# Gated linear attention and an MLP mixer on one core: another hand-over order for the same operations

## The chip, the cores and the metric

The kernel runs on one core of one Trainium2 chip. The metric is device microseconds (us) of one execution. A core has five engines that run side by side, each through its own list of instructions in order: TensorE (PE, matmuls; its weight loads are shown as PEld), ScalarE (ACT), VectorE (DVE), GpSimd (POOL) and SyncE (SP, which mostly issues DMAs). An engine whose next instruction waits for something stands still, and everything behind that instruction in its list stands still with it. Matmul results go to PSUM, which has eight banks; the other engines empty them into SBUF.

## The reference

Four sequences (batches) of 768 rows, 8 heads of width 48. First a gated linear attention, row by row, then an MLP mixer over its result (8 x 48 = 384 columns):

```python
f = 1.0 / (1.0 + np.exp(-f_logit))
for t in range(S):
    state = f[:, :, t, :, None] * state + np.einsum('bhd,bhe->bhde', k[:, :, t], v[:, :, t])
    y[:, :, t] = np.einsum('bhd,bhde->bhe', q[:, :, t], state)

x = y.transpose(0, 2, 1, 3).reshape(B, S, H * D)
h = np.maximum(x.transpose(0, 2, 1) @ w_tok1, 0.0) @ w_tok2       # 768 -> 256 -> 768, over rows
u = x + h.transpose(0, 2, 1)
h2 = np.maximum(u @ w_ch1, 0.0) @ w_ch2                            # 384 -> 1536 -> 384, over columns
out = u + h2
```

## The kernel before

**Tiling.** The 768 rows of a batch are cut into six chunks of 128. Two chunks are worked together (256 rows lie on 128 partitions, two neighbouring rows, j0 and j1, on each), so each batch has three *chunk pairs*, written b.P here: 1.2 is batch 1, chunk pair 2. For a pair the loop over rows becomes a few matmuls and elementwise steps:

1. gates: exp and ln of f on ACT (L449, L451), then `two` (and `two_lo` for b > 0) on DVE (L444)
2. running sums of ln f down a chunk on PE (L473 for b = 0, L475 and L476 after; called *sums*), chunk totals (L480, b = 0); `first` on DVE (L502); four exps of the sums into `GG` on ACT (L505 and L522); end-of-chunk decays (`glast`, L508; or `ends`, L512, and a small transfer on SP, L518)
3. *products*: q and k times `GG`, two per pair, j0 and j1 (L444, `qk<-qk_sb,GG`; DVE, for b = 0 also POOL)
4. *transposes* of the products: for b = 0 and 1 on PE (L550), then copied from PSUM to `qT` and `kT` by ACT or DVE (L430, L432); for b = 2 and 3 by DMA (L535), with a POOL copy (L434)
5. *scores* (L585), masked into `AmT` (DVE in one step, L628; for four tiles of batch 0 an ACT copy, L623, and a POOL multiply, L625)
6. *parts* k times v (L603), which carry the state from chunk to chunk on DVE (L637 to L645); the block-diagonal copy `state_bd` is cast by ACT, DVE or POOL
7. *outs*: state times q (L661) and `AmT` times v (L669) into PSUM, copied to `x_bf` (bf16) and `x_nat` (fp32). For batch 0 the three first `x_bf` tiles are cast late from `x_nat`, on POOL, ACT or DVE.

When a batch's rows are there, the mixer follows: L713 over rows into `h1T` (relu in two halves on ACT or DVE), L729 back, the residual u on DVE (L745), u's bf16 copy `u_bf`, its transposes (L770 on PE, L759 by DMA for b = 2 and 3), copied to `uT`; then the channel mix, L788 into `zT` (24 relus on ACT or DVE, L439 and L441) and L807, the sum (L813) and the store (L706). The mixer of one batch overlaps the attention of the next.

**What sets the order.** The kernel first records 1041 operations, each with the engines that may run it, its inputs and outputs and its PSUM bank. `Plan.best` then walks the table `ORDER` (L23 to L86): a code's quotient by 4 is the operation, its remainder says which of the allowed engines takes it. On the way it computes a planned start for each operation from costs, gives a PSUM bank to each group (the one that has been free longest), and, where PE would stand idle before 25.5 us, puts filler matmuls (L848, on `steady`) into its list. The operations are then emitted by planned start. So the table decides three things: the order in each engine's list, the engine of an operation that has a choice, and the banks. Waits follow from the data: an instruction waits for its inputs, for the readers of what it overwrites, and a group on a bank for those who empty it.

POOL issues the loads of q, k, v and f for the batches ahead (L358) and the weights (L365, L403) from the same list in which it casts and masks; a load that stands behind other work is issued late. At most two buffers hold f, three hold q, k and v.

Of the kernel before, what the change touches and what calls it, by code (L numbers as in the profile page):

```python
# [23 lines left out]
    8, 12, 0, 20, 24, 28, 4, 16, 244, 248, 252, 256, 140, 32, 44, 48, 36, 168, 120, 124, 132, 172, 40, 268, 128,  # L24
    56, 64, 272, 276, 416, 280, 148, 284, 288, 296, 300, 80, 84, 292, 420, 424, 432, 260, 164, 160, 72, 60, 68,
    304, 152, 308, 156, 76, 428, 88, 356, 360, 365, 369, 320, 312, 264, 325, 436, 372, 92, 96, 316, 564, 328,
    332, 376, 444, 448, 384, 380, 340, 568, 572, 580, 584, 588, 452, 348, 456, 336, 352, 100, 468, 473, 576,
    596, 592, 440, 104, 108, 460, 464, 600, 112, 116, 176, 180, 184, 188, 192, 344, 196, 388, 392, 508, 396,
    476, 480, 604, 512, 400, 408, 500, 488, 616, 621, 200, 404, 204, 492, 504, 413, 608, 521, 517, 484, 612,
    764, 524, 624, 628, 528, 532, 536, 496, 636, 632, 644, 648, 768, 736, 652, 740, 540, 544, 548, 656, 664,  # L30
    660, 640, 668, 672, 676, 553, 208, 557, 212, 684, 561, 681, 744, 772, 748, 752, 756, 776, 780, 784, 136,
    789, 760, 872, 856, 840, 844, 860, 876, 808, 812, 824, 828, 792, 796, 865, 848, 880, 920, 928, 816, 832,
    800, 884, 852, 912, 916, 925, 933, 888, 904, 896, 1248, 893, 1252, 836, 908, 820, 900, 1104, 1080, 1040,
    1032, 960, 1036, 1108, 1272, 952, 1044, 944, 1276, 869, 804, 144, 1280, 1284, 1120, 964, 1084, 948, 1125,
    1304, 1308, 1048, 1053, 1056, 1061, 957, 992, 936, 1024, 976, 1000, 1288, 1296, 1292, 1316, 940, 1028, 1312,
    981, 996, 1005, 984, 989, 1320, 1324, 1256, 1260, 1328, 1016, 968, 1096, 1088, 1332, 972, 1100, 1092, 1428,
    1432, 1021, 1436, 216, 1300, 220, 224, 228, 1440, 1460, 1464, 1448, 1444, 1336, 1340, 1344, 1348, 1352,
    1008, 1264, 1012, 1268, 1356, 1360, 1472, 1372, 1364, 1148, 1152, 1072, 1128, 1064, 1468, 1077, 1384, 1484,
    1476, 1112, 1380, 1452, 1068, 1376, 1488, 232, 236, 240, 688, 1588, 1592, 1596, 1604, 1608, 2264, 1368,
    1117, 1480, 1388, 1600, 1132, 1156, 1136, 1400, 1404, 1160, 1140, 1628, 692, 696, 700, 704, 1612, 2268,  # L40
    2288, 1408, 1420, 1424, 1624, 1620, 1412, 1396, 1392, 2272, 1416, 1492, 1496, 1500, 1504, 1508, 1456, 1616,
    1516, 2292, 1528, 1520, 1512, 1632, 1208, 1168, 1172, 1176, 1532, 2296, 1524, 1180, 2276, 2448, 1636, 1644,
    1536, 2304, 2308, 1640, 1544, 2312, 1648, 1540, 1560, 1564, 1212, 2300, 2452, 1548, 708, 712, 716, 720,
    1216, 1652, 1656, 1660, 1664, 1668, 1684, 1680, 1676, 1672, 1576, 1572, 1568, 1804, 1776, 1780, 2456, 1808,
    1784, 1812, 1188, 1552, 1580, 2324, 1556, 1816, 1788, 2320, 2472, 1700, 1704, 1688, 1692, 1696, 1584, 724,
# [836 lines left out]
```

## Time and profile before

| what | us |
|---|---|
| time, median of 3 runs | 168.66 (168.13 to 168.73) |
| the profiled execution, its own time | 168.51 |
| its span in the trace | 166.8 |
| busy: PE, DVE, ACT, POOL | 158.5, 129.3, 106.0, 63.5 |
| the two costliest lines: L807, L788 (both on PE) | 52.1, 50.3 |
| moved by DMA | 24.34 MB, mean 146 GB/s |

The trace names for each instruction its start, its duration, the engine and line, and how long its engine had been idle before it, with whoever ended that. Rows that follow each other without a gap on the same line are shown as one with their count. A row of the table by stretches gives for a stretch of the span the busy time of each engine and the number of its instructions. PE's rows may read as busy without a gap while it waits, because a matmul's end is modelled; the starts are recorded, so a wait shows as a start that comes later than the work before it needs.

The span has three stages: to about 32.8 us the attention of batch 0 and its row mix, with PE short of work; to about 72.2 the channel mix of batch 0 beside the attention of batch 1; then the channel mix of batches 1, 2 and 3 beside the attention of 2 and 3, which ends by about 130.

### The profile page before, as it was taken

What the parts mean: (1) busy time and instruction counts of PE and PEld (TensorE: products, weight loads), DVE (VectorE), ACT (ScalarE), POOL (GpSimd) and SP (SyncE); (2) the same over time, 40 slices, a digit from 0 to 9 for tenths busy, and PEclk for the clock granted to TensorE, in tenths of its full rate; (3) what the DMA queues carried; (4) which work ended last, traced back from release to release, by engine and by line L of the source; (5) the groups of instructions that cost most, each with busy time, mean ns of one, the idle gap of its engine ahead of it and who ended that gap; (6) DMA issues with size and microseconds to landing.
All of it is one profiled execution on the core that took longest, in us unless ns stands there. A gap on an engine that the chain in (4) does not pass through costs nothing.

```text
span 166.8 us, 5023 instructions
## 1 busy us (share of the span) xinstructions
PE 158.5 (95%) x2064; PEld 101.5 (61%) x2064; DVE 129.3 (78%) x287; ACT 106.0 (64%) x228; POOL 63.5 (38%) x87
## 2 busy tenths in 40 slices
PE   5899997899999999999999999999999999999991
PEld 2467865656666666566665766665667566566660
DVE  3499995889899998999999998996699446460331
ACT  3788975789899999976957939386531311725000
POOL 7975899705877200675517003024022022000000
PEclk9999999999999999999999999999999999999998
DMA  5999999999999991599999660985730043600253
GB/s 122 220 177 171 202 211 238 190 233 217 207 221 217 224 238 27 77 162 198 198 199 141 125 165 0 106 158 118 185 120 4 0 98 81 205 0 4 78 194 105
DMA packets 68183, 24.34 MB, mean 146 GB/s; under 512 B 60896, under 2 KB 67296, under 8 KB 68160
## 3 DMA queue, kind: packets, MB, share of 16 engines
q0 software_dynamic: 41856, 13.77, 67.6%
q1 hardware_dynamic: 25776, 10.06, 28.2%
q8 instruction: 16, 0.26, 0.6%
q10 hardware_dynamic: 528, 0.20, 0.4%
q14 instruction: 7, 0.06, 0.1%
HBM read 25.17 MB, written 4.72 MB: 179 GB/s over the span
## 4 chain that ended last, share of the span: by engine, by line
PE 75%; ACT 13%; DVE 5%; issue 2%; DMA 2%; DVEq 0%; ACTq 0%
PE ps L788 27%; PE ps L807 22%; PE ps L729 4%; PE ps L713 4%; PE ps L585 3%; PE ps L669 3%; ACT state_bd L430 2%; PE ps L661 2%; DMA f_sb<-in_f_logit_dram 2%; PE ps L603 2%; ACT f_sb L449 2%; ACT GG L522 2%; PE ps L550 2%; ACT f_sb L451 2%; ACT GG L505 1%
## 5 line engine op out<-in xcount | busy, mean ns | idle before, releaser
L807 PE MATMUL ps<-w_ch,zT 128*128 128x384 bf16 (+2 forms) x300 | 52.1, 320 | 0.4 <-ACT x_nat L430 0.4
L788 PE MATMUL ps<-uT,w_ch 128*128 128x384 bf16 x288 | 50.3, 326 | 0.1
L807 PEld LDWEIGHTS <-zT 128*128 128x128 bf16 x300 | 28.2, 98 | 17.7 <-issue 0.4
L788 PEld LDWEIGHTS <-w_ch 128*128 128x128 bf16 x288 | 27.7, 98 | 17.9 <-issue 0.3
L439 ACT ACTIVATE zT<-ps 128x384 bf16<-128x384 f32 x58 | 26.0, 495 | 16.9 <-PE ps L788 16.7
L628 DVE TENSOR_TENSOR AmT<-ps,mask 128x512 bf16<-128x512 f32 x44 | 28.3, 680 | 1.0 <-PE ps L585 0.8
L441 DVE TENSOR_SCALAR zT<-ps 128x384 bf16<-128x384 f32 x38 | 20.0, 552 | 6.1 <-PE ps L788 6.0
L813 DVE TENSOR_TENSOR x_nat<-x_nat,ps 128x384 f32<-128x384 f32 (+2 forms) x25 | 13.0, 532 | 10.3 <-PE ps L807 10.3
L434 POOL CAST state_bd<-state 48x192 bf16<-48x192 f32 x16 | 5.9, 369 | 33.0 <-DVE state L645 24.3
L444 DVE TENSOR_TENSOR qk<-qk_sb,GG 128x768 bf16<-128x768 bf16 x24 | 13.9, 585 | 1.2 <-ACT GG L522 1.1
L745 DVE TENSOR_TENSOR x_nat<-x_nat,ps 128x384 f32<-128x384 f32 x21 | 10.6, 548 | 3.9 <-PE ps L729 3.9
L358 POOL DMA_DIRECT2D v_sb<-in_v_dram x12 | 10.7, 888 | 5.7 <-DMA w_ch<-in_moe_w_ch_dram 4.9
L505 ACT ACTIVATE GG<-ps 128x384 bf16<-128x384 f32 x24 | 10.8, 488 | 3.1 <-DVE first L502 1.4
L522 ACT ACTIVATE GG<-first 128x384 bf16<-128x384 f32 x24 | 11.8, 520 | 0.6 <-DVE first L502 0.4
L449 ACT ACTIVATE f_sb<-f_sb 128x768 f32<-128x768 f32 x12 | 10.1, 845 | 2.9 <-DMA f_sb<-in_f_logit_dram 2.9
L848 PE MATMUL ps<-steady 128*128 128x512 bf16 x32 | 10.3, 444 | 1.7 <-DVE steady L373 1.7
L434 POOL COPY qT<-qJ 128x1024 bf16<-128x1024 bf16 x5 | 6.0, 1197 | 14.7 <-DMA qJ<-qk 14.6
L358 POOL DMA_DIRECT2D qk_sb<-in_k_dram x12 | 10.8, 900 | 2.0 <-POOLq L866 0.8
L430 ACT ACTIVATE u_bf<-x_nat 128x384 bf16<-128x384 f32 x13 | 6.0, 528 | 8.0 <-DVE x_nat L745 8.0
L358 POOL DMA_DIRECT2D qk_sb<-in_q_dram x12 | 10.6, 887 | 1.3 <-DMA qk_sb<-in_q_dram 0.7
L430 ACT ACTIVATE x_bf<-ps 128x384 bf16<-128x384 f32 x13 | 6.3, 490 | 6.2 <-PE ps L669 4.4
L713 PE MATMUL ps<-x_bf,w_tok 128*128 128x384 bf16 x48 | 10.1, 326 | 0.1
(84 smaller groups left out, 227.8 us busy)
## 6 DMA issues: line engine op xcount, KB each, us to landing
out_dram<-x_nat SPq DMA_DIRECT2D x23, 192.0 KB, 2.2
f_sb<-in_f_logit_dram POOLq DMA_DIRECT2D x9, 384.0 KB, 8.6
qk_sb<-in_k_dram POOLq DMA_DIRECT2D x12, 192.0 KB, 8.7
qk_sb<-in_q_dram POOLq DMA_DIRECT2D x12, 192.0 KB, 8.7
v_sb<-in_v_dram POOLq DMA_DIRECT2D x12, 192.0 KB, 8.8
w_ch<-in_moe_w_ch_dram POOLq DMA_DIRECT2D x2, 576.0 KB, 13.9
w_ch<-in_moe_w_ch_dram POOLq DMA_DIRECT2D x1, 1152.0 KB, 13.1
f_sb<-in_f_logit_dram SPq DMA_DIRECT2D x2, 384.0 KB, 5.6
```

Source lines behind the costliest of these rows:

```text
L358: lambda eng=eng, into=held(dst[i], P), of=runs(src, b, P): eng.dma_start(out=into, in_=of),
L430: nc.scalar.activation(out_, in_, AF.Copy, bias=0.0, scale=1.0)
L439: nc.scalar.activation(out_, in_, AF.Relu, bias=0.0, scale=1.0)
L441: nc.vector.tensor_scalar(out_, in_, 0.0, None, ALU.max)
L444: (nc.vector if op.engine == DVE else nc.gpsimd).tensor_tensor(out_, a, b_, what)
L449: add(ACT, r, lambda: nc.scalar.activation(fb, fb, AF.Exp, bias=0.0, scale=-1.0), make=[key], kind=el, need=([("fb", P)] if P < 1 else []) ...
L522: add(ACT, r, lambda n=n: nc.scalar.activation(GG[i][:, 0, n], banks[p_f.at][:, 0:DM].rearrange("t (h d) -> t h d", d=D) if split else fir ...
L628: add(DVE, r, lambda into=into, made=made, m4=m4: nc.vector.tensor_tensor(into, made(), m4, ALU.mult), need=masks, make=[("AmT", i, js, pa ...
L713: add(PE, rank("tok1", rt), lambda rt=rt, kt=kt, pm=pm: nc.tensor.matmul(banks[pm.at][:, 0:DM], lhsT=w_tok1[:, kt, rt * 128:(rt + 1) * 128 ...
L788: nc.tensor.matmul(banks[pm.at][:, 0:384], lhsT=w[:, kt, c0:c0 + 128], rhs=uT[:, th, :, kt, :], start=(kt == 0), stop=(kt == 2))
L807: nc.tensor.matmul(banks[pm.at][:, 0:n1 - n0], lhsT=zT[:, kt, tt * 128:(tt + 1) * 128], rhs=w_ch2[:, kt, n0:n1], start=(kt == 0), stop=(kt ...
L813: add(DVE, rank("ch2", tt), lambda un=un, pm=pm, n=n1 - n0: nc.vector.tensor_tensor(un, un, banks[pm.at][:, 0:n], ALU.add), make=[("x_nat" ...
```

## The change

Only the table `ORDER` differs, in all its 62 lines: it holds the same 1041 operations, in another order and in part with another choice of engine. A line of it says nothing to a reader:

```diff
 ORDER = (
-    8, 12, 0, 20, 24, 28, 4, 16, 244, 248, 252, 256, 140, 32, 44, 48, 36, 168, 120, 124, 132, 172, 40, 268, 128,
...
+    8, 12, 0, 20, 24, 28, 4, 16, 244, 248, 252, 256, 32, 160, 44, 48, 120, 140, 152, 156, 36, 40, 60, 132, 56,
...
 )
```

The planned starts move with it, and so the fillers: 32 before, 30 now. What each engine's list holds where the prediction speaks of it:

VectorE, the start of batch 0, before (`first_80` and `first_81` belong to chunk pairs 0.0 and 0.1, the two `qk_84` to 0.0's products):

```order
L502 TENSOR_TENSOR first_80<-ps_121,f_sb_74 128x384
L412 MEMSET state_bd_101 128x192
L415 MEMSET qk_84 128x2x8x8 x2
L394 TENSOR_TENSOR mask<-tri_114,ident 64x64 x2
L392 COPY mask<-tri_114 64x128
L444 TENSOR_TENSOR qk_84<-qk_sb_68,GG_82 128x2x8x48
L412 MEMSET state_bd_102 128x192
L444 TENSOR_TENSOR qk_84<-qk_sb_68,GG_82 128x2x8x48
L412 MEMSET state_bd_103 128x192
L396 COPY mask<-tri_114 64x64
L502 TENSOR_TENSOR first_81<-ps_122,f_sb_74 128x384
L637 TENSOR_TENSOR ps_123<-ps_123,glast_94 128x192
```

and now:

```order
L502 TENSOR_TENSOR first_80<-ps_121,f_sb_74 128x384
L415 MEMSET qk_85 128x2x8x8
L396 COPY mask<-tri_114 64x64
L502 TENSOR_TENSOR first_81<-ps_122,f_sb_74 128x384
L444 TENSOR_TENSOR qk_84<-qk_sb_68,GG_82 128x2x8x48 x2
L412 MEMSET state_bd_101 128x192
L637 TENSOR_TENSOR ps_123<-ps_123,glast_94 128x192
```

`first` of 0.1 has moved ahead of both products of 0.0, and the memsets and mask copies between have gone to earlier places. A little further on, 0.1's two products, which had a mask of 0.0 between them, stand one behind the other.

GpSimd, from the first mask multiply of batch 0 on, as a piece of the difference (`qk_84` is now 0.2's product j1; `x_bf_107` are the late casts of batch 0; `qk_sb_69` and `v_sb_72` are loads of q, k and v for 1.0):

```order
 L625 TENSOR_TENSOR AmT_92<-AmT_92,mask 128x512
+L444 TENSOR_TENSOR qk_84<-qk_sb_68,GG_82 128x2x8x48
 L358 DMA qk_sb_69<-in_k_dram 128x8x96
-L358 DMA qk_sb_69<-in_q_dram 128x8x96
-L434 CAST x_bf_107<-x_nat_104 128x384
-L358 DMA v_sb_72<-in_v_dram 128x8x96
+L434 CAST x_bf_107<-x_nat_104 128x384 x2
 L625 TENSOR_TENSOR AmT_93<-AmT_93,mask 128x512 x2
 L625 TENSOR_TENSOR AmT_92<-AmT_92,mask 128x512
+L434 CAST x_bf_107<-x_nat_104 128x384
+L358 DMA qk_sb_69<-in_q_dram 128x8x96
+L358 DMA v_sb_72<-in_v_dram 128x8x96
```

One product has come from DVE to POOL, two casts from ACT, and the loads of q and v of 1.0 now stand behind the masks; w_ch2 and the loads of 1.1, in the same order as before, follow them.

ScalarE, the middle, around the copy of `qT` for the scores of 1.2, before (`f_sb_74` are gates of 2.1, `GG_82` and `ends_97` belong to 2.0, `state_bd` to 1.0 and 1.1, `x_nat_105` to batch 1):

```order
L449 ACTIVATE f_sb_74<-f_sb_74 128x8x96
L430 ACTIVATE x_nat_105<-ps_125 128x384
L451 ACTIVATE f_sb_74<-f_sb_74 128x8x96
L430 ACTIVATE state_bd_103<-state 48x4x48
L505 ACTIVATE GG_82<-ps_124 128x384 x2
L512 ACTIVATE ends_97<-ps_124 128x2x192
L430 ACTIVATE qT_87<-ps_127 128x1024
```

and now:

```order
L449 ACTIVATE f_sb_74<-f_sb_74 128x8x96
L430 ACTIVATE x_nat_105<-ps_122 128x384
L430 ACTIVATE x_bf_108<-ps_122 128x384
L430 ACTIVATE x_bf_108<-ps_127 128x384
L430 ACTIVATE x_nat_105<-ps_127 128x384
L430 ACTIVATE qT_87<-ps_121 128x1024
L430 ACTIVATE state_bd_103<-state 48x4x48 x2
L451 ACTIVATE f_sb_74<-f_sb_74 128x8x96
L430 ACTIVATE state_bd_101<-state 48x4x48
L505 ACTIVATE GG_82<-ps_122 128x384
```

The ln of 2.1, the exps into `GG` and the ends of 2.0, which stood ahead of the copy, stand behind it; the four copies of 1.0's second half, on two other banks, stand ahead of it.

Further, without rows here: on PE, outs of 1.0 stand behind scores and parts of 1.1 and two groups of L807; a group of L807 stands between the last L713 and the first L729 of batch 1; and the third L745 that writes `u_bf` of batch 0 is now the first. The `qT` copy of 1.1 goes from ACT to DVE, the halves of `h1T` of batch 1 change engines, and over the whole program ACT runs 13 operations more than before and DVE 13 fewer. On SP the small transfer of 2.2's ends stands ahead of 2.1's.

110 rows, old and new, of the table ORDER are left out of this document.

## The prediction

> **What bounds the kernel now.** First the page: the span, and who is busy.
>
> ```profile
> span 166.8 us, 5023 instructions
> PE 158.5 (95%) x2064; PEld 101.5 (61%) x2064; DVE 129.3 (78%) x287; ACT 106.0 (64%) x228; POOL 63.5 (38%) x87
> ```
>
> TensorE (PE) bounds the mean, and a mean hides stages. So second, the table by stretches (length; then busy us and instructions of PE, weight load, DVE, ACT, POOL; then granted clock, DMA share, GB/s):
>
> ```profile
> 52.00:72.00 20.00, 19.39 (x337) 13.23 (x336) 19.51 (x44) 19.80 (x45) 6.53 (x8) 1.00 1.12 145
> 72.00:100.00 28.00, 27.90 (x434) 17.79 (x432) 27.07 (x58) 19.68 (x44) 10.89 (x16) 1.00 1.24 171
> 100.00:163.00 63.00, 62.99 (x659) 39.40 (x656) 39.70 (x82) 24.87 (x57) 8.45 (x17) 1.00 0.37 91
> ```
>
> Read it downward. From 100 on PE is full and the others have slack: another order of the same work gains nothing there. From 52 to 72, PE, DVE (19.51 of 20) and ACT (19.80) are all full, so whoever is late stops PE. The clock is full. Third, PE's own timeline, since "busy" counts modelled ends and hides short waits (the bracket is the idle time before a row and who ended it):
>
> ```profile
> 26.02 0.32 PE L669 MATMUL ps<-v_sb,AmT 64*128 64x48 bf16 x11 [1.09 <-issue]
> ...
> 31.17 0.67 PE L770 MATMUL ps<-ident,u_bf 128*128 128x128 bf16 x9
> 32.26 0.68 PE L770 MATMUL ps<-ident,u_bf 128*128 128x128 bf16 x9 [0.43 <-DVE u_bf L745]
> ...
> 53.49 0.46 PE L603 MATMUL ps<-v_sb,qk 64*64 64x48 bf16 x32
> 54.38 2.76 PE L807 MATMUL ps<-w_ch,zT 128*128 128x384 bf16 x16 [0.43 <-ACT x_nat L430]
> ...
> 58.98 1.47 PE L807 MATMUL ps<-w_ch,zT 128*128 128x384 bf16 x8
> 60.45 0.64 PE L585 MATMUL ps<-qT,kT 48*64 48x128 bf16 x32
> 61.26 0.34 PE L661 MATMUL ps<-state_bd,qT 128*128 128x96 bf16 x4
> 61.73 0.65 PE L713 MATMUL ps<-x_bf,w_tok 128*128 128x384 bf16 x3
> ...
> 67.11 2.28 PE L729 MATMUL ps<-h1T,w_tok 128*128 128x384 bf16 x12
> 69.23 1.46 PE L807 MATMUL ps<-w_ch,zT 128*128 128x384 bf16 x8
> ...
> 72.18 0.49 PE L788 MATMUL ps<-uT,w_ch 128*128 128x384 bf16 x2
> ```
>
> One row of the chain prices a 384-wide matmul where PE never waits:
>
> ```profile
> 139.75 10.24 PE ps L788 x63
> ```
>
> 10.24/63 is 0.1625 us. With it the hidden waits come out. Eight matmuls from 58.98 need 1.30, and the next row starts 1.47 later: 0.17 lost. Twelve from 67.11 need 1.95 and take 2.12: 0.17. The four narrow ones from 61.26 take 0.47 to the next row; 128x96 can't need longer than 128x384, so at least 0.47 less 4 x 0.05 (an estimate: a quarter of 0.1625, rounded up) is lost, 0.27. At 54.38 the bracket alone is 0.43. These four are 1.04. Shorter gaps of the same kind between 32.8 and 72.2, at 52 to 65 above all, I put at 0.7 (an estimate: the table has 0.61 of non-busy PE from 52 to 72, of which 0.43 is counted, and as much as the others again is hidden in modelled ends). **So about 1.7 us are lost in the middle, 0.43 at u_bf before it, and 1.09 at a stop for which the profile shows no releaser.** Ahead of these lies a start-up, to 22.7, in which PE is filled up with L848.
>
> **The change, part by part.** Every operation stays; fillers apart (32 before, 30 now) no matmul comes or goes, so what is priced is waiting.
>
> *The start, up to 32.8.* DVE and PE:
>
> ```profile
> 10.63 0.56 DVE L444 TENSOR_TENSOR qk<-qk_sb,GG 128x768 bf16<-128x768 bf16 x1
> ...
> 11.32 0.49 DVE L444 TENSOR_TENSOR qk<-qk_sb,GG 128x768 bf16<-128x768 bf16 x1
> ...
> 12.27 0.56 DVE L502 TENSOR_TENSOR first<-ps,f_sb 128x384 f32<-128x384 f32 x1
> ...
> 13.89 0.69 DVE L432 COPY kT<-ps 128x1024 bf16<-128x1024 bf16 x1
> ...
> 15.23 0.55 DVE L444 TENSOR_TENSOR qk<-qk_sb,GG 128x768 bf16<-128x768 bf16 x1
> ...
> 16.30 0.55 DVE L444 TENSOR_TENSOR qk<-qk_sb,GG 128x768 bf16<-128x768 bf16 x1
> ...
> 30.72 1.48 DVE L745 TENSOR_TENSOR u_bf<-x_nat,ps 128x384 bf16<-128x384 f32 x3
> ```
> ```profile
> 9.42 0.95 PE L480 MATMUL ps<-ones,two 128*128 128x2 f32 x8
> ...
> 11.87 0.43 PE L603 MATMUL ps<-v_sb,qk 64*64 64x48 bf16 x16
> ...
> 17.20 1.05 PE L550 MATMUL ps<-ident,qk 128*128 128x128 bf16 x16
> ...
> 20.41 1.06 PE L550 MATMUL ps<-ident,qk 128*128 128x128 bf16 x16
> ```
>
> (a) `first` of chunk pair 1 (pair 0.1 below: batch 0, pair 1) now stands ahead of 0.0's two products. It needs the end of L480, 9.42 + 0.95 = 10.37, so it runs to 10.9 and the products end near 12.0, not 11.81: L603 comes 0.2 later. The scores of 0.0 wait for the kT copy, to 14.58, where 0.2 is hidden: two state_bd memsets of 0.2 have left this stretch. I take 0 (0 to +0.2). (b) 0.1's products run back to back, ahead of the masks (L628), so the second ends near 16.3, not 16.85, and the transposes wait for PE's own list only: 16.8, not 17.20. That is -0.4. (c) 0.2's product j1 leaves DVE for POOL, and no row has it there. The nearest rows:
>
> ```profile
> 16.59 1.27 POOL L625 TENSOR_TENSOR AmT<-AmT,mask 128x512 bf16<-128x512 bf16 x1 [0.93 <-ACT AmT L623]
> ...
> 20.20 0.50 POOL L434 CAST x_bf<-x_nat 128x384 bf16<-128x384 f32 x1 [0.58 <-ACT x_nat L430]
> ...
> 26.33 0.90 POOL L358 DMA_DIRECT2D f_sb<-in_f_logit_dram  x1
> ```
>
> 768 elements are 1.5 times the 512 of the mask multiply, so 1.9 at its rate; from below, the 0.55 that DVE takes; from above, 3 times the multiply, 3.8, since a strided 8x48 operand may be slower. I take 1.8, a little under the 1.9, since the nearest row is the mask multiply and its three operands are the product's. It starts behind that multiply, at 17.9, and ends at 19.7; the other product, on DVE, ends near 20.0. So the transposes of 0.2 start at 20.05, not 20.41, and the product may take 2.3 (17.9 to 20.2) before anything is later than now. What queues behind it on POOL: the load of k (0.90 as in the row at 26.33), two casts (0.50 each) of which one came from ACT, then the masks of 0.1: 17.9 + 1.8 + 0.9 + 1.0 = 21.6, where they start now as well. So these masks don't move, and OUTS 0.1 behind them doesn't either; of the -0.4 I let 0.1 through. The loads of q and v (1,0), w_ch2 and f (1,1), pushed behind, are a rival. (d) The third u_bf of L745 is now the first, so the transposes of token tile 0 need not wait for 30.72 + 1.48 = 32.20: -0.43, all of it on PE's path. (e) The 1.09 stop waits for nothing in the program; I leave it, at 0 (-1.09 to +1.09). **Start: -0.5** (-0.8 to +0.35 without (e)).
>
> On the page of the Trainium skill that could explain (e), "Runtime: NRT & Kernel Launch", section "Instruction fetch mechanics": programs are fetched in blocks of 16 KiB, and the cost of crossing one is called mostly hidden. By it the stop is worth 0 in both kernels; the row has 1.09, and the measurement decides.
>
> *The middle, 32.8 to 72.2.* The wait at 54.38 is for ACT to empty a bank that OUTS 1.0 (L669) filled just before. That group now stands behind the scores and parts of 1.1 and two groups of L807: two groups of 4 are 1.30, more than the 0.43. The 0.17 at 60.45 is a copy:
>
> ```profile
> 59.38 1.01 ACT L430 ACTIVATE qT<-ps 128x1024 bf16<-128x1024 bf16 x1
> ```
>
> It ends at 60.39, and PE starts at 60.45. Ahead of it on ACT stood an ln, two GG and the ends of 2.x; now they stand behind it, and the scores come as soon as PE is through, near 58.7. For 1.1 the qT copy goes from ACT to DVE: 1.01 there, 0.69 here (the kT row has the same form), so DVE carries 1.38 for 1.1's two copies, under three L807 groups (1.95) that stand between transposes and scores: 0 (0 to +0.3). The 0.27 at 61.26 and the 0.17 at 67.11 waited for x_bf and h1T on ACT; both are split otherwise (h1T's two halves change engines, and a group of L807, 0.65, stands now between L713 and L729): gone. Walked along the new lists with the durations of before, 1.5 of the 1.7 are found again. The walk leaves five places with a lead under 0.2: OUTS 1.0 behind 1.1's last mask, both transposes of 1.2, the sums of 2.1, uT ahead of L788. I charge 0.1 each. **Middle: -1.0** (-1.7, all waits, to +0.3, where the five give back what is won).
>
> *From 72 on.* PE is full; the rows of 72 and 100 leave 0.11 to gain. DVE is 27.07 of 28 up to 100, so a late DVE could cost: **0** (-0.1 to +0.3). On SP one glast transfer of 2.2 passes 2.1's, with a lead of 1.2. Tail: the same.
>
> **Sum: -1.5.** Against the profiled execution, 168.51 (span 166.8 and 1.7 around it), that is **167.0**; the median shown, 168.66, lies 0.15 above it, so the same step gives 167.2 there.
>
> **The rivals.** *A product and POOL at once.* Two rows:
>
> ```profile
> 81.61 1.15 POOL L434 COPY qT<-qJ 128x1024 bf16<-128x1024 bf16 x1 [1.67 <-DMA qJ<-qk]
> ```
> ```profile
> 81.69 1.48 DVE L444 TENSOR_TENSOR qk<-qk_sb,GG 128x768 bf16<-128x768 bf16 x1 [0.18 <-ACT GG L522]
> ```
>
> DVE's product took 1.48 instead of 0.55 while POOL's copy ran, and ended 0.41 after it: it stood still until POOL was done. In the changed order 0.1's second product may fall behind POOL's mask multiply (16.59) in that way: up to 1.27 later, which takes the -0.4 of (b) back. The transposes of 0.1 then start near 17.2 to 17.6, and those of 0.2, for which PE must be free, give up most of what the start gains, 0.4 of the 0.5: 167.4. For: both lists put them near 16.5. Against: the product should start near 15.8, before POOL. The page of the Trainium skill on this is "SBUF — State Buffer", section "Who interferes with whom": DVE and GpSimd share a port pair as an exclusive lock, and the later instruction blocks fully. The pair of rows agrees with it.
>
> *Waits replaced.* The middle is full on three engines; a wait that goes may come back at the next engine. Then only the start and a little remain, -0.3: 168.2. For: 19.80 and 19.51 of 20. Against: ACT's work in the middle falls by 0.9 (one copy of 1.01 leaves).
>
> *The stop goes too,* if it hangs on what lies around it: 165.9. One row can't tell.
>
> *Late load: slower.* Rows:
>
> ```profile
> f_sb<-in_f_logit_dram POOLq DMA_DIRECT2D x1, 384.0 KB, 13.1
> ...
> DMA to landing us min/median/max: 4.4/8.7/13.5
> ```
> ```profile
> 40.40 0.85 ACT L449 ACTIVATE f_sb<-f_sb 128x768 f32<-128x768 f32 x1
> ```
>
> Issued at 26.33, f (1,1) lands 13.1 later, at 39.4, and is used at 40.40. Now it is issued near 30. If the 13.1 is a queue that drains by itself, it lands at 39.4 to 40 all the same, my case; by the median of q and k (second row) at 38.7. If it takes 13.1 from its own issue, it lands at 43.1, 2.7 behind its use. From there PE waits in its order at the sums of 1.1, which stand 0.4 later in the new list: +2.3. It decides from a landing at 40.8; -1.5 + 2.3 gives 169.3, and 0.2 more (an estimate) for k and q of 1.1, which POOL issues behind it, 0.90 each: **169.5**.
>
> *POOL's product slow: slower.* From 2.3 us on each us more is one us later at the transposes of 0.2 and at the masks; at 4.8 it is +2.5, 169.5.
>
> *The order does nothing:* 168.5, if PE's waits are set by loads and the stop alone.
>
> **How the numbers follow.** Forecast 0.48; the product behind POOL 0.12 (0.09 of it faster, 0.03 within); the stop gone too 0.07; waits replaced 0.16; nothing 0.03; late load 0.07; slow product 0.07. About 0.5% (0.84 us) is what a measurement of this kernel tells from no change: against 168.51, faster is below 167.7 and slower above 169.35. Faster 0.48 + 0.09 + 0.07 = 0.64; within 0.16 + 0.03 + 0.03 = 0.22; slower 0.14. The range leaves the two slow cases out and reaches from the case without the stop, 165.9 less 0.2, to 168.5 of no effect and 0.4 for the bounds of (a), (c) and the stretch from 72 on: 165.7 to 168.9.
>
> **What the profile after would show.** Right: the first L603 near 12.1; L550 of 0.1 at or before 16.9; an L444 of 1.8 on POOL near 17.9; the transposes of u_bf without a wait, 31.7; the scores of 1.2 near 58.7; the first L788 of batch 1 near 70.7, not 72.18, and PE full from there; an issue stop of about 1 us near 25.6. Wrong: an L444 on POOL over 2.3; an idle PE that ends on f_sb, k or q near 43; new brackets <-DVE or <-ACT between 50 and 72; a first L788 of batch 1 after 71.7.

## The result, and the profile after

The changed kernel takes 170.49 us (median of 4 runs, 170.11 to 172.59) beside 168.67 (168.13 to 168.73) of the kernel before on the same chip: a ratio of 1.0149 (95% interval 1.0112 to 1.0186). It is slower by 1.8 us. Its profiled execution took 170.36, with a span of 168.7, 1.9 more than before. All ratios here are to the kernel before on the same chip, and leave disturbed executions out, so a median over all executions can lie higher than its ratio says (xnat, below).

The page of the changed kernel, span and engines, then two rows of its table by stretches, with the columns of the one before:

```profile
span 168.7 us, 5008 instructions
...
PE 158.5 (94%) x2058; PEld 101.4 (60%) x2062; DVE 125.1 (74%) x274; ACT 112.1 (66%) x241; POOL 63.4 (38%) x87
```
```profile
52.00:72.00 20.00, 19.66 (x343) 13.34 (x342) 19.30 (x40) 19.60 (x45) 8.36 (x10) 1.00 1.39 176
72.00:100.00 28.00, 26.68 (x428) 17.20 (x427) 24.85 (x56) 23.40 (x54) 9.28 (x13) 1.00 1.05 130
```

PE's work is the same 158.5, so the 1.9 is waiting. The middle is what the forecast wanted: from 52 to 72 PE is at 19.66, not 19.39. But from 72 to 100, where it was full (27.90), it now has 26.68: **1.2 us idle that were not there**. The other part lies ahead of these windows, in the start, where fillers keep PE busy for much of its waiting. PE's timeline has it; rows of the changed kernel, with the idle time before each and its releaser in the bracket:

```profile
8.17 0.91 PE L473 MATMUL ps<-two,tri 128*128 128x384 f32 x2 [0.96 <-DVE two L444]
...
13.43 0.43 PE L603 MATMUL ps<-v_sb,qk 64*64 64x48 bf16 x16
...
18.18 1.05 PE L550 MATMUL ps<-ident,qk 128*128 128x128 bf16 x16
...
27.27 0.30 PE L669 MATMUL ps<-v_sb,AmT 64*128 64x48 bf16 x10 [0.94 <-issue]
...
30.49 2.11 PE L729 MATMUL ps<-h1T,w_tok 128*128 128x384 bf16 x12 [0.25 <-ACT h1T L439]
32.43 1.77 PE L770 MATMUL ps<-ident,u_bf 128*128 128x128 bf16 x18
34.04 1.14 PE L788 MATMUL ps<-uT,w_ch 128*128 128x384 bf16 x6
...
72.71 0.65 PE L788 MATMUL ps<-uT,w_ch 128*128 128x384 bf16 x3
...
91.72 0.24 PE L585 MATMUL ps<-qT,kT 48*64 48x128 bf16 x1
93.10 0.64 PE L585 MATMUL ps<-qT,kT 48*64 48x128 bf16 x31 [1.14 <-ACT x_nat L430]
```

The first L603 starts at 13.43 (11.87 before), L550 of 0.1 at 18.18 (17.20). The first L788 of batch 0 starts at 34.04 (32.77 before). Three marks on PE therefore split the time of every version: the first L788 of batch 0, that of batch 1, and PE's last end.

| us | to L788 of batch 0 | from there to L788 of batch 1 | from there to PE's last end | PE's last end |
|---|---|---|---|---|
| before | 32.77 | 39.41 | 91.00 | 163.18 |
| changed | 34.04 | 38.67 | 92.32 | 165.03 |
| difference | +1.27 | -0.74 | +1.32 | +1.85 |
| predicted | -0.5 | -1.0 | 0 | -1.5 |

**The start.** PE stood 0.96 for `two`, the first of VectorE's pieces of the gate of 0.0. VectorE of the changed kernel ahead of it:

```profile
4.82 0.60 DVE L385 CAST tri<-tri 128x128 bf16<-128x128 f32 x1
5.46 0.23 DVE L394 TENSOR_TENSOR mask<-tri,ident 64x64 bf16<-64x64 bf16 x1
...
5.74 0.55 DVE L392 COPY mask<-tri 64x128 bf16<-64x128 bf16 x1
5.82 0.52 DVE L396 COPY mask<-tri 64x64 bf16<-64x64 bf16 x1
...
6.48 0.69 DVE L392 COPY mask<-tri 64x128 bf16<-64x128 bf16 x1
...
7.56 0.56 DVE L444 TENSOR_TENSOR two<-f_sb 128x384 f32<-128x384 f32 x1
```

and before:

```profile
4.61 0.16 DVE L385 CAST tri<-tri 128x128 bf16<-128x128 f32 x1
6.17 0.56 DVE L444 TENSOR_TENSOR two<-f_sb 128x384 f32<-128x384 f32 x1 [1.41 <-ACT f_sb L451]
...
6.88 0.28 DVE L392 COPY mask<-tri 64x128 bf16<-64x128 bf16 x1
7.02 0.19 DVE L396 COPY mask<-tri 64x64 bf16<-64x64 bf16 x1
...
10.06 0.54 DVE L392 COPY mask<-tri 64x128 bf16<-64x128 bf16 x1
```

Before, VectorE was idle for 1.41 ahead of `two` and wrote the masks after it. In the changed list three mask copies and six other small operations follow the cast in that gap. If the copies took 0.19 to 0.28, as the first two did before, and the cast 0.16, `two` would come some 0.3 later (an estimate: its 6.91 in tt, below, less the 0.44 by which the cast is longer, against 6.17); but the copies take 0.52 to 0.69, the cast of L385 0.60, and `two` starts 1.39 later. (The third of these copies, at 10.06, took 0.54 in the kernel before too, behind `two`.) What was long at the same time stands on POOL, in the changed kernel:

```profile
4.49 0.88 POOL L358 DMA_DIRECT2D qk_sb<-in_k_dram  x1
5.36 0.90 POOL L358 DMA_DIRECT2D qk_sb<-in_q_dram  x1
6.22 0.90 POOL L358 DMA_DIRECT2D v_sb<-in_v_dram  x1
```

The issues of loads end at 5.37, 6.26 and 7.12. The cast ends at 5.42, the next two copies at 6.29 and 6.34, the third at 7.17: each within 0.1 of the end of the issue in which it started. The L394 between them, which reads two tiles, took its 0.23.

**Near 92.** The first score of 2.2 runs at 91.72 and the other 31 stand 1.14, until ACT has emptied a bank (`x_nat`). ACT of the changed kernel, the small transposes by DMA on SP, and the time from the issue of `qJ` to its landing:

```profile
89.40 1.17 ACT L430 ACTIVATE qT<-qJ 128x1024 bf16<-128x1024 bf16 x1 [1.49 <-DMA qJ<-qk]
...
92.57 0.48 ACT L430 ACTIVATE x_nat<-ps 128x384 f32<-128x384 f32 x1
```
```profile
83.80 1.23 SPq L535 DMA_TRANSPOSE qJ<-qk  x1
```
```profile
DMA to landing us min/median/max: 5.5/5.5/5.5
```
```profile
82.32 0.89 POOL L358 DMA_DIRECT2D v_sb<-in_v_dram  x1
83.19 0.90 POOL L358 DMA_DIRECT2D f_sb<-in_f_logit_dram  x1
```

The bank's copy stands on ACT behind the `qT` copy of 2.2 and five others; that copy waits 1.49 for the transpose. Before, POOL made the `qT` copy of 2.2, at nearly the same time, and no bank waited behind it:

```profile
89.20 1.22 POOL L434 COPY qT<-qJ 128x1024 bf16<-128x1024 bf16 x1
```

The transpose took 5.5 to land, while two loads, of 192 and 384 KB, had gone out within 1.5 us ahead of it.

### The profile page after: what moved, and what is told of

Its sections match the earlier page's. It is cut to its first block, busy times and chain, and to the rows that moved or that the text cites. A ratio compares the mean times of both kernels' runs of the same rounds, so it can differ in the third digit from the quotient of the medians.

```text
span 168.7 us, 5008 instructions
## 1 busy us (share of the span) xinstructions
PE 158.5 (94%) x2058; PEld 101.4 (60%) x2062; DVE 125.1 (74%) x274; ACT 112.1 (66%) x241; POOL 63.4 (38%) x87
## 3 DMA queue, kind: packets, MB, share of 16 engines
q1 hardware_dynamic: 25776, 10.06, 27.8%
## 5 line engine op out<-in xcount | busy, mean ns | idle before, releaser
L807 PE MATMUL ps<-w_ch,zT 128*128 128x384 bf16 (+2 forms) x300 | 52.0, 320 | 0.0
L788 PE MATMUL ps<-uT,w_ch 128*128 128x384 bf16 x288 | 50.5, 326 | 0.2 <-DVE zT L441 0.2
L788 PEld LDWEIGHTS <-w_ch 128*128 128x128 bf16 x288 | 27.6, 98 | 18.0 <-issue 0.2
L807 PEld LDWEIGHTS <-zT 128*128 128x128 bf16 x300 | 28.0, 98 | 16.9
L439 ACT ACTIVATE zT<-ps 128x384 bf16<-128x384 f32 x62 | 27.9, 500 | 10.7 <-PE ps L788 10.5
L441 DVE TENSOR_SCALAR zT<-ps 128x384 bf16<-128x384 f32 x34 | 17.7, 549 | 6.9 <-PE ps L788 6.9
L813 DVE TENSOR_TENSOR x_nat<-x_nat,ps 128x384 f32<-128x384 f32 (+2 forms) x25 | 13.2, 533 | 11.2 <-issue 5.9
L434 POOL CAST state_bd<-state 48x192 bf16<-48x192 f32 x14 | 5.1, 364 | 30.1 <-DVE state L645 18.1
L745 DVE TENSOR_TENSOR x_nat<-x_nat,ps 128x384 f32<-128x384 f32 x21 | 10.6, 548 | 5.5 <-PE ps L729 5.4
L430 ACT ACTIVATE x_nat<-ps 128x384 f32<-128x384 f32 x20 | 9.5, 490 | 7.4 <-DVE x_bf L432 5.1
L444 DVE TENSOR_TENSOR qk<-qk_sb,GG 128x768 bf16<-128x768 bf16 x23 | 12.3, 553 | 1.6 <-ACT GG L522 1.1
L449 ACT ACTIVATE f_sb<-f_sb 128x768 f32<-128x768 f32 x12 | 10.2, 847 | 1.7 <-DMA f_sb<-in_f_logit_dram 1.7
L848 PE MATMUL ps<-steady 128*128 128x512 bf16 x26 | 9.0, 498 | 1.7 <-DVE steady L373 1.7
L451 ACT ACTIVATE f_sb<-f_sb 128x768 f32<-128x768 f32 x12 | 10.2, 848 | 0.2
L713 PE MATMUL ps<-x_bf,w_tok 128*128 128x384 bf16 x48 | 10.2, 327 | 0.0
```

The source lines that it names most:

```text
L430: nc.scalar.activation(out_, in_, AF.Copy, bias=0.0, scale=1.0)
L439: nc.scalar.activation(out_, in_, AF.Relu, bias=0.0, scale=1.0)
L441: nc.vector.tensor_scalar(out_, in_, 0.0, None, ALU.max)
L444: (nc.vector if op.engine == DVE else nc.gpsimd).tensor_tensor(out_, a, b_, what)
L713: add(PE, rank("tok1", rt), lambda rt=rt, kt=kt, pm=pm: nc.tensor.matmul(banks[pm.at][:, 0:DM], lhsT=w_tok1[:, kt, rt * 128:(rt + 1) * 128 ...
L788: nc.tensor.matmul(banks[pm.at][:, 0:384], lhsT=w[:, kt, c0:c0 + 128], rhs=uT[:, th, :, kt, :], start=(kt == 0), stop=(kt == 2))
```

## The experiments

Each edit is made in the changed kernel unless it says otherwise; "H" stands for the held copies, "Q" for the queue on ACT.

**tt: the three mask copies, in their places, as a product of a tile with itself** (0 and 1 stay 0 and 1).

```diff
-nc.vector.tensor_copy(mask[r, 0], tri2[r, r].unsqueeze(2).broadcast_to((64, 64, 2)))
+nc.vector.tensor_tensor(mask[r, 0], *[tri2[r, r].unsqueeze(2).broadcast_to((64, 64, 2))] * 2, ALU.mult)
-nc.vector.tensor_copy(mask[r, 1, :, 1], tri2[r, r])
+nc.vector.tensor_tensor(mask[r, 1, :, 1], tri2[r, r], tri2[r, r], ALU.mult)
```

> The changed order with the mask copies of L392 and L396 written as a multiply of the 0/1 triangle by itself (same values, same place in the list). Theory H (held copies): three copies of the start end within 0.1 us of the end of a load issue on POOL, so they were held by it, and a two-input operation will not be. Then `two` of 0.0 starts at 6.4 to 6.8 instead of 7.56, the first L603 near 12.4, the span falls by 0.8 to 1.1 to about 167.7, the time to about 169.4. Theory N (the list ahead of `two` is simply too long by its own work): a multiply costs no less than a copy, `two` stays at 7.3 to 7.6 and the span within 0.3 of 168.7.

169.60 us, 1.0064 (1.0039 to 1.0089). VectorE of this kernel:

```profile
5.73 0.22 DVE L392 TENSOR_TENSOR mask<-tri 64x128 bf16<-64x128 bf16 x1
5.88 0.21 DVE L396 TENSOR_TENSOR mask<-tri 64x64 bf16<-64x64 bf16 x1
...
6.23 0.29 DVE L392 TENSOR_TENSOR mask<-tri 64x128 bf16<-64x128 bf16 x1
...
6.91 0.56 DVE L444 TENSOR_TENSOR two<-f_sb 128x384 f32<-128x384 f32 x1
```

Same places, same sizes, same issues beside them: 0.21 to 0.29 instead of 0.52 to 0.69, and `two` comes 0.65 earlier (6.91, 0.1 behind the range expected), L788 of batch 0 0.69 (33.35). The number of operations in the list is the same, so 0.65 of the 1.39 is not their count, it is the kind of these three. The cast at 4.81 was left and still took 0.60.

**late: the three copies behind the first L502.**

```diff
-... 36, 40, 60, 132, 56, 64, 164, 68, 124, 168, 128, 268, 72, 272, 276, 416, 280, 172, ...
+... 36, 40, 60, 132, 164, 124, 168, 128, 268, 72, 272, 276, 416, 280, 56, 64, 68, 172, ...
```

> The changed order with three mask copies (L392 twice, L396) moved behind the first L502, all else as it is. Theory H (held copies): `two` of 0.0 starts at 6.1 to 6.3, as its input is there at 6.0; span -1.2 to -1.4, time near 169.1. Theory N (own work): the copies' own times as they stand undisturbed in the kernel before, 0.28 + 0.19 + 0.28, come off: `two` at 6.8, span -0.75, time near 169.6. In both the rest of the loss (the stop at L585 near 92) stays.

169.16 us, 1.0044 (1.0013 to 1.0075). VectorE and POOL:

```profile
6.22 0.56 DVE L444 TENSOR_TENSOR two<-f_sb 128x384 f32<-128x384 f32 x1
...
9.05 0.73 DVE L392 COPY mask<-tri 64x128 bf16<-64x128 bf16 x1
9.18 0.64 DVE L396 COPY mask<-tri 64x64 bf16<-64x64 bf16 x1
9.84 0.23 DVE L392 COPY mask<-tri 64x128 bf16<-64x128 bf16 x1
```
```profile
8.80 0.93 POOL L358 DMA_DIRECT2D v_sb<-in_v_dram  x1
9.67 0.88 POOL L403 DMA_DIRECT2D w_tok<-in_moe_w_tok_dram  x1
```

`two` is back at 6.22 and L788 of batch 0 starts at 32.73: all 1.31 of the start came back. Two copies are still held where they now stand, to 9.78 and 9.82, when an issue ends at 9.73. The third begins 0.17 after the next issue, of L403, and takes 0.23: it is not held. Nobody needs VectorE yet where they stand. The traces of all kernels divide in this way: mask copies and the cast of L385 that begin 0.24 or more after an issue's beginning last to its end, those that begin up to 0.22 after it do not. The stop near 92 stays, at 0.47.

**xnat: on ACT, the `x_nat` copy ahead of the `qT` copy of 2.2.**

```diff
-    for op in plan.best(idle, 6500.0, 25500.0):
+    seq = plan.best(idle, 6500.0, 25500.0)
+    seq.remove(plan.ops[611])
+    seq.insert(seq.index(plan.ops[669]), plan.ops[611])
+    for op in seq:
```

> The changed order with one ACT copy (x_nat of 2.0's second chunk, L430) handed over ahead of the qT copy of 2.2 instead of five places behind it. Theory Q: the stop of 1.14 in L585 near 92 is the wait for the bank that this copy empties, and the copy was late because ACT stood 1.49 at the qT copy, which waits for a transpose by DMA. Then the stop goes, the L585 of 2.2 runs through from 91.7, and the span falls by 1.1 to 1.4 to about 167.4, time near 169.1. Rival R: the scores of 2.2 wait for the transposed q and k anyway, or PE stops there for no releaser as it does near 26: the stop stays at 0.8 or more and the span within 0.3.

170.23 us, 1.0072 (1.0042 to 1.0102), 169.32 in the profiled execution; its times scatter, from 169.32 to 174.55. The scores of 2.2 on PE no longer stop:

```profile
92.10 0.64 PE L585 MATMUL ps<-qT,kT 48*64 48x128 bf16 x32
```

The stretch from L788 of batch 1 on is 91.30, against 92.32, although the scores of 2.1 now wait 0.33 for a transpose (`kT`). So the second half of the loss hung on the order of these two copies on ACT.

**both: late and xnat together.**

> Both moves together (the three mask copies behind the first L502, and the one x_nat copy ahead of the qT copy). If the two losses are the whole of the slowdown and independent: span -2.4 to -2.7 against the changed order, about 166.1, time near 167.9, a ratio to the kernel before of 0.994 to 0.998; what is left of the gain is then the 0.74 of the middle. If one loss hides behind the other or a new wait takes their place: ratio 1.000 or more.

168.55 us, 0.9997 (0.9974 to 1.0020). The expected gain did not come. The start is 32.73 and the last stretch 91.42, as wanted; the middle went up to 39.62. ACT and PE of this kernel:

```profile
42.46 0.84 ACT L449 ACTIVATE f_sb<-f_sb 128x768 f32<-128x768 f32 x1 [0.99 <-DMA f_sb<-in_f_logit_dram]
```
```profile
44.61 0.41 PE L585 MATMUL ps<-qT,kT 48*64 48x128 bf16 x15 [0.35 <-ACT zT L439]
```

With the start repaired, the gates of 1.1 were needed before they had landed, and what is queued on ACT behind that L449 (`zT`) stops PE. In the changed kernel itself ACT came to the same L449 only at 42.67, without a wait: the delay of the start had hidden the late load, the prediction's rival.

**fload: both, and the load of f (1,1) issued ahead of q and v of 1.0 and `w_ch2`.** In the list of moves, as in xnat: op 53 goes ahead of op 50.

> As the kernel with both moves, and POOL issues the load of f (1,1) ahead of those of q and v (1,0) and w_ch2 instead of behind them. In the profile of both moves f (1,1) is issued near 30.2, lands at 42.4 and is used at once, and PE stops 0.56 near 44 (a relu of ACT stands behind the exp that waits for f) and 0.31 near 50. Theory L (the late load is what eats the middle's gain once the start is mended): f lands by 37, both stops go, the span falls by 0.5 to 0.9 to 166.5 to 166.9, time near 168.0. Rival: these stops hang on the order of ACT's list and come whenever f lands: span within 0.2 of 167.4.

168.66 us, 0.9990 (0.9960 to 1.0020). Half right: the middle is 38.68 again (33.01 to 71.69) and the stop is gone, but the start is 0.28 later (the stop at L669 without a releaser took 1.22, not 0.93) and the last stretch 0.40 longer than in both. PE ends 0.26 earlier in the profiled executions, and the times don't tell the two apart.

**sp: both, and the transpose of `kT` of 2.1 ahead of the small transfers of L518 on SP** (op 624 ahead of op 660).

> As the kernel with both moves, and on SP the second transpose by DMA of 2.1 (into kT, L535) ahead of the two small transfers (L518) that stand between the two transposes, 1.9 us. Theory S: the scores of 2.1 (L585 near 85.4, 0.48 late there) wait for kT by that: they start at 85.0 and the span falls by 0.3 to 0.5, time near 168.2. Rival: they wait for the POOL copy into qT, which ends later than kT lands: no change (within 0.2).

168.44 us, 0.9987 (0.9960 to 1.0015): no difference. The scores of 2.1 now run through (84.84), yet those of 2.2 stop for 0.34, this time on an `x_nat` of VectorE (L813).

**fill and all: the thirteen first fillers as 52 of 128 columns.** The stop of 0.94 without a releaser (27.27) ended no wait that the profile shows. Counted along PE's rows of matmuls and weight loads it stood behind the 697th to the 704th in all ten kernels with uncut fillers (in three of them, the changed one too, four fillers have no row, which makes 697 there 701), at 24.75 to 26.15 us: it kept its number and not its time. So `fill` is both with 78 more instructions on PE and the same work ahead of it; `all` is the same with the moves of fload and sp.

```diff
-        for _ in range(n):
-            nc.tensor.matmul(banks[NBANK - 1], lhsT=steady[:, 0:128], rhs=steady, start=True, stop=True)
+        w = 128 if n == 13 else 512
+        for _ in range(n * 512 // w):
+            nc.tensor.matmul(banks[NBANK - 1][:, 0:w], lhsT=steady[:, 0:128], rhs=steady[:, 0:w], start=True, stop=True)
```

> As the kernel with both moves, and each of the 13 first filler matmuls (before 7.2 us) cut into four of 128 columns, 78 PE instructions more and no more work. The stop without a releaser near 26 comes behind PE's instruction 700 to 704 in all six traces, wherever that falls in time. Theory F (it hangs on the number of instructions, as when the next block of the program is fetched): it comes again behind instruction 700 to 704, now 78 earlier in the program, in the last L603 of batch 0 near 23.8, and L669 of 0.1 runs through; since PE waits there for masks until 24.3 anyway, the span falls by 0.2 to 0.6. Rival W (it is a wait of that L669): it stays in the middle of L669 of 0.1 and nothing else changes.

> All five edits together (mask copies behind the first L502, the x_nat copy ahead of the qT copy, f (1,1) ahead of the loads before it, kT's transpose ahead of the small transfers, the first fillers cut in four). If each gives what its theory says: span 165.6 to 166.2, time 167.3 to 167.9, ratio to the kernel before 0.992 to 0.996. If the gains don't add, no better than the best of the others.

fill took 172.35 in its profiled execution (172.35 to 177.44 over four), all 173.59, 1.0270 (1.0227 to 1.0312). PE of fill, with the stop's place and the price:

```profile
24.78 0.58 PE L669 MATMUL ps<-v_sb,AmT 64*128 64x48 bf16 x32
...
91.95 0.42 PE L585 MATMUL ps<-qT,kT 48*64 48x128 bf16 x16 [2.19 <-ACT qT L430]
92.74 0.21 PE L585 MATMUL ps<-qT,kT 48*64 48x128 bf16 x1 [0.37 <-ACT zT L439]
94.03 0.64 PE L585 MATMUL ps<-qT,kT 48*64 48x128 bf16 x15 [1.08 <-DVE x_nat L813]
...
95.01 1.14 PE L788 MATMUL ps<-uT,w_ch 128*128 128x384 bf16 x3
```
```profile
94.00:96.00 2.00, 1.97 (x35) 1.41 (x35) 1.86 (x5) 1.14 (x3) 1.90 (x3) 0.50 0.15 6
```

The stop is gone from L669; behind PE's 701st row, now in an L603 at 23.76, the next matmul starts 0.23 later, which is what is left of it. The start is 31.83, 0.90 earlier than in both, as a theory of the instruction's number wants. Everything behind came earlier too, the transpose of 2.2 (issued 82.48) met the load of f (82.81), and landed after 8.2 (in all, 10.5, in an execution of 175.88, its longest). PE stood 2.19, 0.37 and 1.08, and then the granted clock of the second view was 0.50: three L788 took 1.14, not 0.65. An earlier start, and a time that is 3.8 worse.

**ld3: the changed kernel with the loads of v (3.1) and f (3.2) issued at 73.5 and 74.4 instead of 82.3 and 83.2** (ops 439 and 440 ahead of op 600). The lists of PE, VectorE and ACT stay as they are.

> The changed order, and POOL issues two loads for batch 3 (v of 3.1 and f of 3.2) eight us earlier, behind the q load ahead of them, so that they don't stand beside the transposes by DMA of 2.2 (issued 82.3 and 83.2, the transpose 83.8; it lands 5.5 us later, where 3.0 to 3.7 is the rule). Theory C (collision): the transpose of 2.2 lands in 3.0 to 4.0, the qT copy of ACT ends 1.5 to 2.4 sooner, x_nat behind it empties its bank in time, the stop of 1.14 at L585 near 92 goes: span -0.9 to -1.3, to about 167.6, although no compute engine's list has changed. Rival O (the order of ACT's list alone made the stop): the transpose lands as late as before (over 5), the stop stays, span within 0.3 of 168.7.

169.61 us, 1.0052 (1.0017 to 1.0087). PE:

```profile
86.38 0.64 PE L585 MATMUL ps<-qT,kT 48*64 48x128 bf16 x32 [0.91 <-DMA kT<-qk]
...
92.68 0.64 PE L585 MATMUL ps<-qT,kT 48*64 48x128 bf16 x32
```

The transpose of 2.2 lands after 3.2, and its scores run through, with `x_nat` still behind `qT` on ACT: so an earlier landing also removes the stop, and moving the loads gave one here. But the transposes of 2.1 now land after 4.3 and 5.0 and its scores wait 0.91, though no load was issued near them. The last stretch is 91.68, a gain of 0.64 of 1.32.

**bfill: the kernel before with the fillers cut alone.**

> The kernel before, with each of its 13 first filler matmuls cut into four of 128 columns (78 PE instructions more, no more work). If the stop without a releaser hangs on the instruction's number (it did not come in the middle of L669 with the same edit to the changed order): L669 of 0.1 runs through, the stop falls among L603, L585 or L713 ahead of it where PE waits for others anyway, and the first L788 comes 0.6 to 1.2 earlier; span -0.4 to -1.0, ratio 0.994 to 0.998. If being early costs at the later transposes by DMA, as there: ratio 1.00 or above.

168.43 us, 0.9979 (0.9951 to 1.0006). PE:

```profile
24.72 0.40 PE L603 MATMUL ps<-v_sb,qk 64*64 64x48 bf16 x13 [0.57 <-issue]
...
76.21 0.64 PE L585 MATMUL ps<-qT,kT 48*64 48x128 bf16 x32 [1.21 <-DMA kT<-qk]
```

The stop has moved ahead in the program, from L669 to an L603, and shrunk from 1.09 to 0.57; the start gains 0.27, less than expected (its first L603 comes 0.51 later, at 12.38), and a new wait of 1.21 for a transpose of 2.0 takes it.

**five: the moves of late, xnat, fload, sp and ld3 together; best2: five with the fillers cut.**

> The changed order with mask copies late, x_nat ahead of the qT copy, f (1,1) ahead, kT's transpose ahead of the small transfers, and the two loads of batch 3 early. Theory C: the scores of 2.2 run through, span 166.4 to 166.9, time 168.0 to 168.4, ratio 0.995 to 0.998. Otherwise as the kernels with four of these edits: 168.4 to 168.7.

> The five edits and the first fillers cut in four. Theory C: the loss of over 4 us near 90 that came with the cut fillers was the transposes of 2.2 landing 8.2 to 10.5 us after issue beside the load of f; with the loads away they land in under 4.5, PE runs through, and the 1.2 of the start is kept: span 165.2 to 165.9, time 166.9 to 167.6, ratio 0.989 to 0.994. Rival: the loss comes back with another cause: ratio 1.01 or above.

five takes 167.56 us (167.28 to 167.96), 0.9926 (0.9895 to 0.9957), best2 166.70 (166.54 to 168.79), 0.9919 (0.9880 to 0.9958). Both beat the two kernels. The twelve times of best2 fall in two groups, near 166.6 and near 168.4; its profiled execution is of the upper one, and has a stop of 0.55 at the scores of 2.2, where five has none: there the transpose landed after 4.8, in five after 3.2, with the loads as early. In that execution the first load of f landed at 5.13, not at 4.2 to 4.5 as in all the others, and `two` started at 6.91. How much the moves of the loads and transposes alone would have given in the order before was not tried, so five does not show that the new order is the better one.

The stages of the versions side by side, from one profiled execution each (those of both, sp and bfill took 0.5 to 0.8 more than the median of their kernel, that of best2 2.1 more; all is left out):

| us | to L788 of batch 0 | to L788 of batch 1 | to PE's last end | PE's last end |
|---|---|---|---|---|
| tt | 33.35 | 38.67 | 92.20 | 164.22 |
| late | 32.73 | 39.05 | 92.06 | 163.84 |
| xnat | 34.02 | 38.68 | 91.30 | 164.00 |
| both | 32.73 | 39.62 | 91.42 | 163.77 |
| fload | 33.01 | 38.68 | 91.82 | 163.51 |
| sp | 33.48 | 38.67 | 91.74 | 163.89 |
| fill | 31.83 | 38.67 | 96.49 | 166.99 |
| ld3 | 34.02 | 38.68 | 91.68 | 164.38 |
| bfill | 32.50 | 39.41 | 91.84 | 163.75 |
| five | 32.75 | 38.67 | 90.89 | 162.31 |
| best2 | 32.64 | 38.67 | 92.14 | 163.45 |

In the changed order the middle is 38.67 wherever the load of f (1,1) is in time, and 39.05 or 39.62 where it is not. A start varies between executions too: up to batch 0's L788 sp has the same lists as both, and is 0.75 later, since the 13 fillers took 5.73, not 4.44, and the stop at L669 1.17, not 0.93. The last stretch scatters by 1.3 without fill; waits for transposes are part of that.

## Why the prediction was wrong

The forecast was faster by 1.5; it is slower by 1.85 in the profiled executions. By its own steps:

- **(a), the start, is the step that failed first.** It priced `first` of 0.1 ahead of 0.0's products at 0 to +0.2, and began its account at 10.37. It took the end of L480, 9.42 + 0.95, from the trace of before, though the memsets and mask copies that the order's rows show as "gone to earlier places" went ahead of `two`, the head of that chain. It counted them as a relief of this stretch and nowhere as a load on the other. `two` came 1.39 later, the first L603 1.56 (13.43, not 11.87). tt and late show the cause: with the three copies rewritten `two` comes 0.65 earlier, with them moved 1.34, to 6.22, though the memsets still stand ahead of it. So the three copies are 1.33 of the 1.56: 0.65 because they are held (in tt the first L603 starts at 12.78), the rest because they stand there at all. The 0.23 that stays in late is the 0 to +0.2 that (a) had priced.
- **(b) and (c) hold, behind (a).** Without the held copies (late) the first L603 starts at 12.10 (predicted 12.1) and L550 of 0.1 at 16.88 (16.8, mark 16.9). The product on POOL took 1.64, its start 18.00 in late (1.8 and 17.9 predicted), and the masks follow at 21.54 (21.6). The rivals of a slow product and of a product behind POOL are out (0.1's second product began at 16.82, ahead of the mask multiply at 17.21, and took 0.54). But the transposes of 0.2 come at 20.67, not 20.05: PE was held inside the scores of 0.1, whose 32 matmuls took 1.18 there and 0.71 before. The gain of 0.36 was lost at a step that had not been priced; what held the scores was not traced.
- **(d) was wrong in kind.** The bracket at `u_bf` is gone, as foretold, and the time is not: the 18 transposes from 32.43 to 34.04 take 1.61, and two times the 0.51 of nine (32.26 to 32.77 before) are 1.02. Some 0.59 of waiting is inside the row, in four pieces, the longest of them, 0.22, up to the end of the last L745 (33.38): the transposes still wait for each `u_bf` in turn. And 0.25 came new at `h1T`. From the run of eight L713 to L788 it was 5.17 before (27.60 to 32.77), and is 5.27 (28.77 to 34.04). So in late, where the held copies are away, (a) to (e) together gave -0.04 (32.73 against 32.77) instead of -0.5.
- **(e)** stayed, 0.94 for 1.09, as taken.
- **The middle: right in mechanism, off in size.** -1.0 forecast, -0.74 measured, in every version whose loads are in time. The copy's 0.17 ahead of the scores of 1.2 is gone, as foretold: ACT's `qT` ends at 60.44, and the scores start at 60.95, 0.09 after the eight L807 from 59.56 are through, a step that L807 or L788 to L585 takes elsewhere as well (0.09 at 93.55 before). What was not priced is a new wait for ACT, a bracket of the kind that the prediction named as a sign of being wrong:

```profile
65.29 0.34 PE L713 MATMUL ps<-x_bf,w_tok 128*128 128x384 bf16 x1
65.97 0.33 PE L661 MATMUL ps<-state_bd,qT 128*128 128x96 bf16 x4 [0.34 <-ACT state_bd L430]
```

One L713 needs 0.1625, so 0.52 is lost there; every other kernel in the new order loses 0.51 or 0.52 at that place. It is more than the 0.26 that is missing. The four waits that the prediction had counted, 1.04 in all, are gone; the shorter gaps that it put at 0.7 were not measured.
- **"From 72 on: 0 (-0.1 to +0.3)" is the second step that failed.** It read a full PE as proof that nothing could go wrong, and gave late engines 0.3. It is +1.32: 36.48 against 35.49 from L788 of batch 1 to that of batch 2 (+0.99), and 0.33 behind it, which are two matmuls (one L475, one L476, 2 x 0.1625) that have moved past this mark. The stop is the larger part of it, and longer than its bracket, which counts from a modelled end: two scores start 0.02 apart elsewhere, and here 1.38, so 1.36. A new wait of 0.25 at 97.85 (L788, for `zT` of VectorE) adds to it, and two of before that are gone (0.26 at 88.61, 0.14 inside the scores from 84.56) take away. Together that is 1.21 of the 1.32; 0.11 was not traced. The cause of the stop is one copy that went from POOL to ACT and waits there for a transpose that lands at 89.3, with a bank's copy queued behind it that PE needs. xnat takes the stop away at the queue, ld3 by the landing: either half is enough. The prediction followed SP's list and found a lead of 1.2 there; it did not ask what ACT holds back while it waits for that landing.
- **Late load.** f (1,1) was issued at 31.47 (near 30 predicted) and landed 10.2 later, at 41.7: past the threshold of 40.8, and not at the 39.4 to 40 that the forecast took. It cost nothing only because the start was late too, with the use at 42.67. both shows the price once the start is early: 0.95 of the middle (39.62 against 38.67), below the 2.3.
- **Waits replaced** was near the truth in mechanism, in the wrong place: the middle kept its gain, and the start and the stretch from 72 on gave back more.

Of slower by over 0.5% the prediction made 0.14, all of it for two mechanisms that did not decide; the two that did were not among its rivals. One was in reach of its own page: the Trainium skill, "SBUF — State Buffer", section "Who interferes with whom", which it cited for products, says in the same section that copies and casts can run in a mode that uses the port pair which VectorE shares with GpSimd, and then contend with it, while a `tensor_tensor` takes only the pair's read side and the writing of DMA descriptors needs the write side (the page calls this last part inferred). The trace agrees where the copy began 0.24 or more after the issue: copies of 0.52 to 0.73 that end with an issue, and 0.21 to 0.29 for the same work as `tensor_tensor`.

What stays open: why `qJ` of 2.2 lands after 3.2 to 8.2 (loads beside it go with the long ones, but it took 4.8 without any in best2), and the two groups of best2, of which only the upper was profiled. That the stop without a releaser hangs on the instruction's number is supported by the kernels with more instructions ahead of it (fill, bfill and best2, 0.20 at 24.79); what is done at that number was not tried apart, nor why it is shorter there.

## What to carry to other kernels

When operations move earlier, price them where they arrive, on the list ahead of the first thing that the next engine waits for, and at the duration that they have beside what runs there: here a copy of 0.2 on VectorE from SBUF to SBUF that began 0.24 or more after the beginning of POOL's issue of a load ended when that issue did. When a copy that waits for a DMA changes engine, list what is then queued behind it on the new engine, and whether the next engine needs any of it. A gain in one stage moves all later transfers against each other: repairing the start alone gave 1.31 there and brought a late load to light, and of the kernels in the new order only those that moved loads and copies together (five, best2) were faster than the one before, five at 0.9926.

## What the runs showed of the hardware

- VectorE's mask copies and its cast of L385, 0.16 to 0.23 us when undisturbed, took up to 0.74 when they began 0.24 or more after the beginning of a DMA issue of POOL (0.88 to 0.93 each): those that would have ended inside it ended within 0.1 of its end. Those that began up to 0.22 after it were not held (0.16 for the cast at 4.61, the issue in the kernel before from 4.49; 0.23 at 9.84 in late, the issue from 9.67). Copies out of PSUM were not held either: two `state_bd` casts from 20.59 in the kernel before took 0.72 together and ended at 21.31, beside an issue from 20.65 to 21.53.
- The transpose by DMA of 2.2 into `qJ` landed after 3.2 where the last load had been issued 9 us and more ahead (five, ld3; 4.8 in best2), after 4.9 to 5.5 with a 384 KB load issued 0.6 ahead of it (changed, tt, late, xnat, both, fload, sp), and after 8.2 with that load issued 0.3 behind it (fill).
- PE stopped for 0.93 to 1.22 behind its 697th to 704th row for no wait that the profile shows, in ten kernels, and for 0.20 and 0.57 near there with more instructions ahead (best2, bfill). The Trainium skill, "Runtime: NRT & Kernel Launch", section "Instruction fetch mechanics", calls the crossing of a block of instructions mostly hidden; if that is what is seen here, it was not hidden.
- After 3.64 us of idle PE between 89.8 and 94.0 the granted clock was 0.50 from 94 to 96 (fill), in a stretch in which the changed kernel has 1.00.
